# Where and in which tiles the sums of xT's quarters are made, at the seam between expert 0 and expert 1

## The chip, the cores and the metric

One core of a Trainium2 chip. The metric is the device time of the whole program in microseconds (us), lower is better. Most executions of one kernel agree within 0.3%.

## The reference

Attention with exponential features makes x (4608 x 512). A router turns x into weights P by eight alternating normalisations, and eight experts add to the output:

```python
logits = x @ w_gate
P = np.exp(logits - logits.max())
for _ in range(8):
    P /= P.sum(1, keepdims=True) + 1e-09
    P /= P.sum(0, keepdims=True) + 1e-09
    P *= N / E
out = 0
for e in range(8):
    out += P[:, e:e+1] * (np.maximum(x @ w1[e], 0) @ w2[e])    # D = 512, F = 1024
```

## The kernel before

The tokens lie in nine groups of 512. Expert 0 is computed while the attention ends and while the router runs, in plain products; its result, still without P, lies in `acc`. Experts 1 to 7 use a scheme with seven in place of eight quarter products. It needs sums of quarters: sums of the weights (once per expert), "X sums" of xT, which is x transposed (once per group, the same for all experts), and "S sums" of the hidden values hT (each group, each expert). A small scheduler written in Python inside the kernel fixes the order of every engine's instructions before the program is built. It books modelled durations, takes buffers from rings of tiles, and always issues what can start first. So a change in a ring or in a duration can move any instruction of any engine.

The X sums are made once, at the seam between expert 0 and expert 1, written to DRAM, and read back for every expert and group:

```python
ring("s_p", [128, 4, 256], BF16, "S", 5)        # S sums of hT
ring("s_p", [128, 2, 2, 256], BF16, "X", 3)     # X sums, and their reloads

def sub(eng, el, out_, x, y, op, r, w):         # dve = VectorE, pool = GpSimd
    f = nc.vector if eng is dve else nc.gpsimd
    eng(..., lambda: f.tensor_tensor(out=out_(), in0=x(), in1=y(), op=op), r, w)

def sums_x(g):
    X = [new("X") for _ in range(2)]            # two of the three X tiles
    ...
    for n, y, z, r in ((0, b12, b11, []), (1, b22, x(0), [0]), (2, b22, b12, []), (3, b21, x(1), [1])):
        sub(dve if g < 6 else pool, 512, x(n), y, z, ALU.subtract, ...)
    for i in range(2):
        dma("SP", ..., out=Xd[g][i], in_=X[i]())

def load_x(g):                                  # for every expert and group
    X = [new("X") for _ in range(2)]
    for i in range(2):
        dma("SP", ..., out=X[i](), in_=Xd[g][i])
```

The router's serial chain, eight times, nearly all on VectorE with one tiny product on TensorE:

```python
u  = L * c                        # DVE, from the second time on
rr = 1 / u.sum(experts)           # DVE reduce, DVE reciprocal
wv = L * rr                       # DVE
cs = wv.sum(tiles)                # DVE reduce
pc = colw.T @ cs                  # TensorE, 8 columns
c  = 1 / pc                       # DVE
# after the eighth: P = wv * c    # DVE
```

TensorE's second product on a bank (a buffer in which products add up) waits until ScalarE has copied the first one's partial sum out (`U`, an `activation` copy). And before expert 1 adds to a group, ScalarE must scale what expert 0 left there, four "rescales" for each of nine groups:

```python
def keep(fp, n):                                # TensorE waits for this U copy
    act(512, lambda: nc.scalar.copy(out=u[fp][n](), in_=x[fp]()), [x[fp]], [u[fp][n]])
...
if e == 1:
    for ts in range(4):                         # the rescales: can start once P is there
        act(512, lambda ts=ts: nc.scalar.activation(
            out=acc[g][:, ts, :], in_=acc[g][:, ts, :], func=ACT.Copy, bias=0.0,
            scale=P[:, 4 * g + ts, 0:1]), ["P", ("acc", g, ts)], ...)
```

## Time and profile before

| what | before |
|---|---|
| median of the first three runs | 1064.5 us (1063.76 to 1066.44) |
| span of the profiled run | 1064.0 us |
| TensorE busy, page | 96% |
| routing weights P (start of the last routing instruction) | 264.21 us |
| first product of expert 1 | 274.36 us |
| TensorE without work, 275 to 345 us | 7.83 us (70.00 - 62.17) |

The windows of the kernel before show the span cut into stages: for each engine the busy time in the window and the number of instructions, then the granted TensorE clock (1.00 is full speed), the DMA share and GB/s. PE is TensorE, PEld its weight loads, DVE VectorE, ACT ScalarE and POOL GpSimd.

```profile
core 0: us, PE busy (x) PEld busy (x) DVE busy (x) ACT busy (x) POOL busy (x), PEclk, DMA share, GB/s
225.00:240.00 15.00, 12.69 (x96) 6.20 (x95) 10.39 (x23) 2.62 (x6) 9.31 (x8) 0.89 0.19 71
240.00:275.00 35.00, 34.79 (x170) 16.76 (x172) 27.32 (x61) 19.81 (x34) 0.98 (x2) 1.00 0.34 83
275.00:290.00 15.00, 12.72 (x106) 9.94 (x105) 9.30 (x15) 15.00 (x30) 1.09 (x2) 1.00 0.53 89
290.00:305.00 15.00, 12.73 (x113) 10.75 (x112) 14.12 (x20) 13.08 (x28) 12.91 (x10) 1.00 0.32 107
305.00:325.00 20.00, 17.38 (x144) 14.50 (x143) 14.94 (x27) 9.97 (x22) 7.74 (x6) 0.91 0.31 102
325.00:345.00 20.00, 19.34 (x179) 17.18 (x177) 16.67 (x32) 11.47 (x25) 6.30 (x5) 1.00 0.21 71
...
345.00:960.00 615.00, 615.00 (x5636) 551.02 (x5634) 475.71 (x848) 386.07 (x806) 265.09 (x211) 1.00 0.27 62
```

From 345 to 960 us TensorE has no gap at all: nothing that frees another engine there can shorten the run. The gaps lie at the seam. What TensorE waited for between 275 and 345 us (line waited for, total, times, longest):

```profile
PE P_5744 L983 <- DVE S L896: 2.0, 1, 2.0
PE P_5553 L983 <- DVE S L896: 1.7, 1, 1.7
PE P_5208 L983 <- ACT U L1011: 0.8, 1, 0.8
...
```

Two S sums on VectorE are 3.7 us of it, about half of the 7.83 us without work. What VectorE did ahead of the first (its timeline: start, length, line, operation, tiles, shapes):

```profile
291.46 1.06 DVE L896 TENSOR_TENSOR X<-xT 128x512 bf16<-128x512 bf16 x1
...
293.23 1.50 DVE L896 TENSOR_TENSOR X<-xT,X 128x512 bf16<-128x512 bf16 x1
...
299.23 2.56 DVE L896 TENSOR_TENSOR S<-hT 128x1024 bf16<-128x1024 bf16 x2
```

Four X sums stand in front of expert 1's own work, and the first and the last of them take 1.06 and 1.50 us in place of 0.42. The two S sums take 2.56 us in place of the usual 1.28. GpSimd was busy with work that reads two inputs in both stretches; at 296 to 301 us that was its own four X sums, of which this is the last:

```profile
299.65 1.60 POOL L896 TENSOR_TENSOR X<-xT,X 128x512 bf16<-128x512 bf16 x1
```

Ahead of the second wait, the X sums can be read in the chain of work that ended last (start, length, engine, tile, line): four X sums, the last three of them shown, run just before the S sums that TensorE waits for. There they take their usual time, 1.33 us of the chain.

```profile
313.20 1.00 DVE X L896 x3
314.21 0.79 DVE acc_78 L1087 x2
314.99 1.21 DVE S L896 x2
316.25 1.06 PE P_5744 L983 x8
```

The second S-sum wait has a sequel. TensorE's timeline (in brackets: idle before, and what ended it):

```profile
316.25 1.05 PE L983 MATMUL P_5744<-w_3852,S 128*128 128x256 bf16 x8 [2.00 <-DVE S L896]
317.92 1.67 PE L983 MATMUL P_5735<-T,S 128*128 128x256 bf16 x7 [0.62 <-ACT V L1097]
319.39 1.06 PE L983 MATMUL P_5766<-xT,w_3831 128*128 128x256 bf16 x4
```

After the wait four products take 1.06 us where they otherwise take 0.60. In one-microsecond windows the granted clock is 0.50 from 318 to 321 us.

### The profile page before, as it was taken

To read this page: it belongs to the slowest core of one execution; us is meant where nothing else is said; L and a number is where in the kernel's file an instruction comes from. 1 tells how busy PE (TensorE), PEld (TensorE's weight loads), DVE (VectorE), ACT (ScalarE), POOL (GpSimd) and SP (SyncE) were. 2 spreads that over 40 slices of the span, in tenths; PEclk is the share of its full clock that TensorE was granted. 3 is DMA by queue.
4 is the path that set the end of the run, shared out by engine and by line. 5 is a ranking of instruction groups with operands and counts; after the bars stand their busy time and mean duration, and the time that the engine had idled before them with its cause. 6 is when DMAs were issued, how large, how long until landed. Compare 5 with 4: busy or idle time off the path is not lost.

```text
span 1064.0 us, 24542 instructions
## 1 busy us (share of the span) xinstructions
PE 1021.8 (96%) x9498; PEld 842.4 (79%) x9536; DVE 834.4 (78%) x1628; ACT 711.4 (67%) x1568; POOL 496.8 (47%) x567
## 2 busy tenths in 40 slices
PE   6789999999989999999999999999999999999997
PEld 3456666654668888888888888888888888888886
DVE  6889989978697788877867887778777777787775
ACT  5799989944965666566666666666666665666664
POOL 8775756450163444443443443444443444334434
PEclk9999999999999999999999999999999999999999
DMA  9998986812531144113411251116111621114332
GB/s 144 152 179 136 136 143 120 139 41 70 90 130 60 41 90 87 44 41 80 90 41 48 53 110 50 41 50 120 41 41 41 114 57 50 41 42 128 121 118 119
DMA packets 104948, 91.57 MB, mean 86 GB/s; under 512 B 45312, under 2 KB 80256, under 8 KB 104832
## 3 DMA queue, kind: packets, MB, share of 16 engines
q1 hardware_dynamic: 64752, 63.78, 21.9%
q0 software_dynamic: 40080, 26.23, 18.3%
q8 instruction: 74, 1.21, 0.5%
q14 instruction: 42, 0.34, 0.1%
HBM read 94.98 MB, written 14.16 MB: 103 GB/s over the span
## 4 chain that ended last, share of the span: by engine, by line
PE 86%; DVE 5%; ACT 4%; issue 2%; POOL 2%; DMA 1%; ACTq 0%; DVEq 0%; POOLq 0%
DVE m L376 1%; DVE S L896 1%; DMA qk_r<-in_q_dram 1%; DVE xb L590 0%; DVE X L896 0%; ACT U L1011 0%; ACT V L1097 0%; POOL X L896 0%; PE P_6471 L983 0%; PE P_6315 L983 0%; PE P_5735 L983 0%; PE P_16154 L983 0%; PE P_12150 L983 0%; PE P_11799 L983 0%; PE P_8771 L983 0%
## 5 line engine op out<-in xcount | busy, mean ns | idle before, releaser
L983 PEld LDWEIGHTS <-S 128*128 128x128 bf16 x2016 | 197.1, 98 | 31.9 <-DVE S L896 5.9
L983 PEld LDWEIGHTS <-T 128*128 128x128 bf16 x1512 | 147.9, 98 | 19.4 <-issue 2.0
L983 PEld LDWEIGHTS <-hT 128*128 128x128 bf16 x1512 | 147.8, 98 | 18.4 <-DVE hT L1015 1.0
L896 DVE TENSOR_TENSOR S<-hT 128x1024 bf16<-128x1024 bf16 x126 | 85.8, 717 | 0.0
L1100 POOL TENSOR_TENSOR acc_4737<-acc_4737,V 128x512 f32<-128x512 f32 x28 | 35.8, 1284 | 54.7 <-ACT V L1097 54.3
L1100 POOL TENSOR_TENSOR acc_80<-acc_80,V 128x512 f32<-128x512 f32 x28 | 35.5, 1273 | 55.2 <-ACT V L1097 54.7
L1100 POOL TENSOR_TENSOR acc_79<-acc_79,V 128x512 f32<-128x512 f32 x28 | 37.3, 1337 | 51.1 <-ACT V L1097 50.6
L1100 POOL TENSOR_TENSOR acc_77<-acc_77,V 128x512 f32<-128x512 f32 x28 | 35.8, 1289 | 52.7 <-ACT V L1097 52.4
L1100 POOL TENSOR_TENSOR acc_4740<-acc_4740,V 128x512 f32<-128x512 f32 x28 | 35.8, 1288 | 49.5 <-ACT V L1097 49.4
L1100 POOL TENSOR_TENSOR acc_78<-acc_78,V 128x512 f32<-128x512 f32 x28 | 37.2, 1336 | 45.6 <-ACT V L1097 45.5
L1100 POOL TENSOR_TENSOR acc_4738<-acc_4738,V 128x512 f32<-128x512 f32 x28 | 35.6, 1276 | 46.0 <-ACT V L1097 45.4
L1100 POOL TENSOR_TENSOR acc_81<-acc_81,V 128x512 f32<-128x512 f32 x28 | 35.6, 1275 | 45.1 <-ACT V L1097 44.4
L1100 POOL TENSOR_TENSOR acc_4739<-acc_4739,V 128x512 f32<-128x512 f32 x28 | 35.7, 1283 | 43.8 <-ACT V L1097 43.3
L384 PEld LDWEIGHTS <-hT 128*128 128x128 bf16 x288 | 27.6, 100 | 23.5 <-issue 2.2
L896 DVE TENSOR_TENSOR S<-hT,S 128x1024 bf16<-128x1024 bf16 x63 | 46.0, 730 | 0.2
L896 DVE TENSOR_TENSOR S<-S,hT 128x1024 bf16<-128x1024 bf16 x63 | 44.1, 701 | 0.8
L384 PEld LDWEIGHTS <-w_449 128*128 128x128 bf16 x288 | 26.1, 99 | 23.4 <-issue 2.9
L384 PEld LDWEIGHTS <-qkT 128*128 128x128 bf16 x256 | 23.8, 100 | 20.7 <-DVE xb_r L595 4.4
L983 PEld LDWEIGHTS <-w_3831 128*128 128x128 bf16 x288 | 28.7, 99 | 5.1 <-issue 1.1
L983 PEld LDWEIGHTS <-w_5136 128*128 128x128 bf16 x288 | 28.2, 98 | 3.3
L983 PEld LDWEIGHTS <-w_13108 128*128 128x128 bf16 x288 | 28.2, 98 | 3.3
L983 PEld LDWEIGHTS <-w_11506 128*128 128x128 bf16 x288 | 28.2, 98 | 3.3
(4013 smaller groups left out, 3303.2 us busy)
## 6 DMA issues: line engine op xcount, KB each, us to landing
v_m<-in_v_dram SPq DMA_DIRECT2D x15, 512.0 KB, 4.6
qk<-in_k_dram POOLq DMA_DIRECT2D x15, 256.0 KB, 4.9
qk<-in_q_dram POOLq DMA_DIRECT2D x15, 256.0 KB, 5.7
X<-xd_98 SPq DMA_DIRECT2D x7, 256.0 KB, 2.6
X<-xd_99 SPq DMA_DIRECT2D x7, 256.0 KB, 2.7
X<-xd_100 SPq DMA_DIRECT2D x7, 256.0 KB, 2.6
X<-xd_101 SPq DMA_DIRECT2D x7, 256.0 KB, 2.7
X<-xd_102 SPq DMA_DIRECT2D x7, 256.0 KB, 2.6
```

Source lines behind the costliest of these rows:

```text
L376: dve(el, lambda: nc.vector.tensor_reduce(out=dst(), in_=src(), axis=AX.X, op=ALU.max, apply_absolute_value=True), r, w)
L384: nc.tensor.matmul(out_, lhsT=lhsT, rhs=rhs, start=start, stop=stop)
L896: lambda: f.tensor_tensor(out=out_(), in0=x(), in1=y(), op=op), r, w, **kw)
L983: pe(256, lambda i=i, k=k, z=z: nc.tensor.matmul(bank()[:, 256 * i:256 * i + 256], lhsT=lhs(k, i), rhs=rhs(k), start=first and z, stop=k = ...
L1100: pool(670, lambda: nc.gpsimd.tensor_tensor(out=acc[g][:, 2 * i:2 * i + 2, 256 * j:256 * j + 256], in0=acc[g][:, 2 * i:2 * i + 2, 256 * j: ...
```

## The change

The intent: make the X sums in the five S tiles, which nobody needs before the first S sums of expert 1, so that the sums need not share three tiles with their own reloads; and make all of them on VectorE, where one takes 0.42 us alone, against 1.15 us on GpSimd. The core of the diff (shortened):

```diff
     def sums_x(g):
-        X = [new("X") for _ in range(2)]
+        X = [new("S") for _ in range(2)]
         def x(n):
-            return lambda: X[n // 2]()[:, n % 2]
+            return lambda: X[n // 2]()[:, n % 2 * 2:n % 2 * 2 + 2]
         ...
-            sub(dve if g < 6 else pool, 512, x(n), y, z, ALU.subtract,
+            sub(dve if g in (0,1,2,3,4,5,6,7,8) else pool, 512, x(n), y, z, ALU.subtract,
```

The cut parts of the diff give names to choices that stay as they were (a tenth group, expert 0's quarters, a plain product for the last group: all switched off), and write 18 of ScalarE's copies as activations with scale 1.0.

More of the change, by code (lines that the diff above doesn't have):

```diff
@@ L682, in akey @@
     def akey(g):
-        return ["late"] if g >= NA else []
+        return ["late"] * (g >= NA) + ["P"] * (g >= 9)
     def up0(g, part):
@@ L694, in down0, with keys @@
         py = down(W[0][1], hts[g], tss, akey(g))
+        def keys(ts):
+            return [("acc", g, ts)] + [("acc", g, ts, j) for j in range(2) if g >= 9]
         for i, ts in enumerate(tss):
             if ts % 2:
-                act(512, lambda i=i, ts=ts: nc.scalar.copy(
-                    out=acc[g][:, ts, :], in_=py()[:, 512 * i:512 * i + 512]),
-                    [(py, i)] + akey(g), [("acc", g, ts)])
-            else:
-                dve(512, lambda i=i, ts=ts: nc.vector.tensor_copy(
-                    out=acc[g][:, ts, :], in_=py()[:, 512 * i:512 * i + 512]),
-                    [(py, i)] + akey(g), [("acc", g, ts)])
+                act(512, lambda i=i, ts=ts: nc.scalar.activation(
+                    out=acc[g][:, ts, :], in_=py()[:, 512 * i:512 * i + 512], func=ACT.Copy,
+                    bias=0.0, scale=P[:, 4 * g + ts, 0:1] if g >= 9 else 1.0),
+                    [(py, i)] + akey(g), keys(ts))
+            else:
+                dve(512, lambda i=i, ts=ts: nc.vector.tensor_scalar_mul(
+                    out=acc[g][:, ts, :], in0=py()[:, 512 * i:512 * i + 512],
+                    scalar1=P[:, 4 * g + ts, 0:1]) if g >= 9 else nc.vector.tensor_copy(
+                    out=acc[g][:, ts, :], in_=py()[:, 512 * i:512 * i + 512]),
+                    [(py, i)] + akey(g), keys(ts))
     halves, rests, W = {}, {}, {}
@@ L745, in expert0 @@
     def expert0(i):
-        if i < 0 or i >= 40:
+        if i < 0 or i >= (4 * (0 or NG) + 4):
             return
         plan.prio = 0
-        if i < 36:
+        if i < (4 * (0 or NG)):
             up0(i // 4, i % 4)
@@ L866, with store @@
         expert0(i)
-    def store(g, ts):
-        if g < 8:
+    def store(g, ts, one=0):
+        if one:
+            dma('SP', 1 << 18, 320, lambda: nc.sync.dma_start(
+                out=out[g * S:g * S + SM].rearrange('(p j) d -> p j d', j=NJ)[:, ts:ts + 1],
+                in_=acc[g][:, ts:ts + 1, :]),
+                [('acc', g, ts, j) for j in range(2)], [('out', g, ts)])
+        elif g < 8:
             if ts % 2:
@@ L898, in sums_w @@
     def sums_w(e, w1, w2):
+        eng = pool if e == 0 else dve
         def q(w, i, j):
@@ L905, in k @@
         def k(w, i, j):
-            return [(w, i, j)]
+            return [(w, i, j)] if e else [(w, n) for n in range(4)]
         S = [None] + [new("T") for _ in range(3)]
@@ L919, in sums_w @@
         late = ["late"] + (["P"] if e == 1 else [])
-        sub(dve, 1024, s(2), q(w1, *a11), q(w1, *a21), ALU.subtract,
+        sub(eng, 1024, s(2), q(w1, *a11), q(w1, *a21), ALU.subtract,
             k(w1, *a11) + k(w1, *a21) + late, [S[2]])
-        sub(dve, 1024, q(w1, *a21), q(w1, *a21), q(w1, *a22), ALU.add,
+        sub(eng, 1024, q(w1, *a21), q(w1, *a21), q(w1, *a22), ALU.add,
             k(w1, *a22) + late, k(w1, *a21))
-        sub(dve, 1024, s(1), q(w1, *a21), q(w1, *a11), ALU.subtract,
+        sub(eng, 1024, s(1), q(w1, *a21), q(w1, *a11), ALU.subtract,
             k(w1, *a21) + k(w1, *a11) + late, [S[1]])
-        sub(dve, 1024, s(3), q(w1, *a12), s(1), ALU.subtract,
+        sub(eng, 1024, s(3), q(w1, *a12), s(1), ALU.subtract,
             k(w1, *a12) + [S[1]] + late, [S[3]])
         b11, b12, b21, b22 = (0, 0), (0, 1), (1, 0), (1, 1)
-        sub(dve, 1024, t(2), q(w2, *b22), q(w2, *b12), ALU.subtract,
+        sub(eng, 1024, t(2), q(w2, *b22), q(w2, *b12), ALU.subtract,
             k(w2, *b22) + k(w2, *b12) + late, [T[2]])
-        sub(dve, 1024, q(w2, *b12), q(w2, *b12), q(w2, *b11), ALU.subtract,
-            k(w2, *b11) + late, k(w2, *b12))
-        sub(dve, 1024, t(1), q(w2, *b22), q(w2, *b12), ALU.subtract,
-            k(w2, *b22) + k(w2, *b12) + late, [T[1]])
-        sub(dve, 1024, t(3), q(w2, *b21), t(1), ALU.subtract,
+        t1, t1k = q(w2, *b12), k(w2, *b12)
+        if 0 and e == E - 1:
+            T[0] = new("T")
+            t1, t1k = t(0), [T[0]]
+        sub(eng, 1024, t1, q(w2, *b12), q(w2, *b11), ALU.subtract,
+            k(w2, *b11) + k(w2, *b12) + late, t1k)
+        sub(eng, 1024, t(1), q(w2, *b22), t1, ALU.subtract, k(w2, *b22) + t1k + late, [T[1]])
+        sub(eng, 1024, t(3), q(w2, *b21), t(1), ALU.subtract,
             k(w2, *b21) + [T[1]] + late, [T[3]])
@@ L940, in sums_w @@
         Bq = {"11": (q(w2, *b11), k(w2, *b11)), "21": (q(w2, *b21), k(w2, *b21)),
-              "22": (q(w2, *b22), k(w2, *b22)), "t1": (q(w2, *b12), k(w2, *b12)),
+              "22": (q(w2, *b22), k(w2, *b22)), "t1": (t1, t1k),
               "t2": (t(1), [T[1]]), "t3": (t(2), [T[2]]), "t4": (t(3), [T[3]])}
@@ L947, in xq @@
         return lambda: xT[:, 2 * i:2 * i + 2, 512 * g + 256 * j:512 * g + 256 * j + 256]
-    Xd = [[dram.tile([128, 2, 2, 256], BF16, name=f"xd{g}{i}") for i in range(2)]
+    Xd = [[dram.tile([128, 4, 256], BF16, name=f"xd{g}{i}") for i in range(2)]
           for g in range(NG)]
     def sums_x(g):
-        X = [new("X") for _ in range(2)]
+        X = [new("S") for _ in range(2)]
         def x(n):
-            return lambda: X[n // 2]()[:, n % 2]
+            return lambda: X[n // 2]()[:, n % 2 * 2:n % 2 * 2 + 2]
         b11, b12, b21, b22 = xq(g, 0, 1), xq(g, 0, 0), xq(g, 1, 1), xq(g, 1, 0)
@@ L972, in load_x @@
         for i in range(2):
-            dma("SP", 1 << 18, 250, lambda i=i: nc.sync.dma_start(out=X[i](), in_=Xd[g][i]),
+            dma("SP", 1 << 18, 250, lambda i=i: nc.sync.dma_start(out=X[i]().rearrange("p a b c -> p (a b) c"), in_=Xd[g][i]),
                 [("Xd", g, i)], [X[i], "order of X"])
@@ L1022, in relu @@
                 func=ACT.Relu, bias=0.0, scale=1.0), [x[fp]], [(hT[i], fp, j)])
-        more = [("banks", fp) for fp in range(2)]
+        more = [("banks", 0), ("banks", 1)]
         more += [k for n in ("s2", "s3", "22") for k in A[n][1]] + X + list(r0)
@@ L1039, in w1 @@
         def w1(fp):
-            prod(w, fp, "s1", "t1", True, A["s4"][1] + list(r0), hT, [("banks", fp)])
+            prod(w, fp, "s1", "t1", True, A["s4"][1] + r0, hT, [("banks", fp)])
         def x3(fp):
@@ L1057, in up7, with acc_part, down8 @@
             for fp in range(2)}
+    def acc_part(g, i, j):
+        return lambda: acc[g][:, 2 * i:2 * i + 2, 256 * j:256 * j + 256]
+    def down8(e, g, hT, w2):
+        for ts in (2, 3, 0, 1):
+            py = new("P1")
+            for fc in range(8):
+                i, j = fc // 4, ts // 2
+                pe(512, lambda py=py, ts=ts, fc=fc: mm(
+                    py(), hT[fc // 4]()[:, fc % 4, ts * 128:ts * 128 + 128], w2()[:, fc, :],
+                    fc == 0, fc == 7), [(hT[i], fp, j) for i in range(2) for fp in range(2)]
+                    + [(w2, i, j) for i in range(2) for j in range(2)] + ["P"], [py])
+            dve(580, lambda py=py, ts=ts: nc.vector.scalar_tensor_tensor(
+                out=acc[g][:, ts, :], in0=py(), scalar=P[:, 4 * g + ts, e:e + 1],
+                in1=acc[g][:, ts, :], op0=ALU.mult, op1=ALU.add),
+                [py, "P"], [("acc", g, ts, j) for j in range(2)])
+            store(g, ts, 1)
     def down7(e, g, hT, B7):
@@ L1066, in hk @@
             return [(hT[j], fp, i) for fp in range(2)]
+        late, seen = akey(g), set()
         S = [new("S") for _ in range(4)]
@@ L1080, in prod, with start @@
             product(bank, lambda k, i: lhs()[:, k, 128 * i:128 * i + 128],
-                    lambda k: f()[:, k, :], 4, r + r2 + ["P"] + list(more), first)
+                    lambda k: f()[:, k, :], 4, r + r2 + (["P"] if e else late) + list(more), first)
+        def start(bank, i, j):
+            out_ = acc_part(g, i, j)
+            w = [("acc", g, 2 * i + n, j) for n in range(2)]
+            if (i, j) in seen:
+                dve(500, lambda: nc.vector.tensor_tensor(
+                    out=out_(), in0=bank().rearrange("p (a b) -> p a b", a=2), in1=out_(),
+                    op=ALU.add), [bank] + late, w)
+            else:
+                act(512, lambda: nc.scalar.copy(
+                    out=out_(), in_=bank().rearrange("p (a b) -> p a b", a=2)),
+                    [bank] + late, w)
+            seen.add((i, j))
         def read(bank, i, j):
+            if e == 0:
+                return start(bank, i, j)
             for n in range(2):
@@ L1093, in read2 @@
         def read2(bank, i, j):
+            if e == 0:
+                return start(bank, i, j)
             u = new("V")
@@ L1103, in read2 @@
                 [(u, 0), (u, 1)], [("acc", g, 2 * i + n, j) for n in range(2)])
-        if e == 1:
+        if e == 1 and g < 9:
             for ts in range(4):
@@ L1108, in down7 @@
                     out=acc[g][:, ts, :], in_=acc[g][:, ts, :], func=ACT.Copy, bias=0.0,
-                    scale=P[:, 4 * g + ts, 0:1]), ["P", ("acc", g, ts)],
+                    scale=P[:, 4 * g + ts, 0:1]), ["P", ("acc", g, ts)] + akey(g),
                     [("acc", g, ts, j) for j in range(2)])
@@ L1150 @@
     dn = None
-    for e in range(1, E):
-        w1, w2 = load_w(e, [("xT", 5, 3)])
-        if e == 1:
-            for g in range(NG):
+    for e in range(0 if 0 else 1, E):
+        w1, w2 = load_w(e, [("xT", 5, 3)]) if e else W[0]
+        if e == (0 if 0 else 1):
+            for g in (0,1,2,3,4,5,6,7,8):
                 sums_x(g)
         A7, B7 = sums_w(e, w1, w2)
-        for g in (list(range(NG)) if e < E - 1 else [8] + list(range(8))):
+        for g in (range(0, NG) if e == 0 else range(NG) if e < E - 1 else [8, *range(8)]):
             X = load_x(g)
@@ L1167 @@
                 dn["out"]()
-            dn = down7(e, g, hT, B7)
-    for n in ORDER:
-        if len(n) == 2:
-            dn[n]()
-    dn["out"]()
+            if 0 and e == E - 1 and g == 7:
+                down8(e, g, hT, w2)
+            else:
+                dn = down7(e, g, hT, B7)
+    if not 0:
+        for n in ORDER:
+            if len(n) == 2:
+                dn[n]()
+        dn["out"]()
     plan.run(tc)
```

## The prediction

> **What bounds the kernel now.** The busy table gives TensorE 96%, and from 340 us to 1050 us the windows show it busy without a gap. Time can be won only at the seam (225-345), where expert 0 and the serial routing chain end and expert 1's seven-product scheme begins. There the windows show:
> - TensorE idle 7.8 us between 275 and 340: 2.3 in 275-290, 2.3 in 290-305, 2.6 in 310-320, 0.7 in 335-340.
> - A granted clock of 0.77 and 0.89 in 315-325, an estimated 1.7 us more.
>
> ScalarE is busy without a pause from 265 to 295: it rescales acc in 36 instructions, 0.62 us apart, once the routing weights P are ready (264.7). TensorE's waits there name ScalarE's U copies (0.8, 0.6 us), then the S sums on VectorE (1.7 and 2.0 us). Just before these, VectorE did X sums for later groups; beside GpSimd's X sums at 296-301 two S sums took 2.56 us in place of 1.28. The Trainium skill (SBUF — State Buffer, "Who interferes with whom") says that two-input VectorE instructions contend with GpSimd's reads; the trace agrees.
>
> **What changes.** No arithmetic is added. Much of the diff is dead here (`down8`, a tenth group, expert 0's quarters). What counts:
> - 12 X sums leave GpSimd (1.15 to 1.28 us each) for VectorE (0.42 us, 0.34 apart): +4 us of VectorE.
> - The sums no longer wait for the three X tiles that reloads hold. In the built order all 36 stand inside the routing chain, before P; 16 stood between 291 and 334. From the eighth on, the write-outs go out with no reload between them.
>
> **Cost.** The chain gets 28 more VectorE sums before P. Interleaved with dependent routing steps, one costs an estimated 0.2 us beyond the spacing (two sums between reduce, reciprocal and product make it 1.25 in place of 0.90), so about 6 us, less idle gaps of some 5 us. But TensorE's tiny column-sum products stand later in its stream: the eighth comes 26 products of 0.216 us later, so P comes at about 270 in place of 264.7. Expert 0's fill keeps TensorE busy till 275 either way; only 8 rescales, in place of 15, are done before expert 1 starts. The other 28 mix with the U copies; at 21 such the loss was 2.3 us (275-290), so an estimated 3 to 3.5 us now. For waits for S tiles I allow 0.5 us.
>
> **Gain.** The S-sum waits of 300-305 and 310-320 and the clock dip (1.7 + 2.6 + 1.7 us), and some of the 0.7 at 335, go nearly all: about 6 us. Net about 4.5 us. TensorE's last 1237 rows keep their order, so the tail stays.
>
> **Prediction:** 1060.0 us, 8 in 10 within 1055.5 to 1065.0. Faster by over 2%: 0.01; within 2%: 0.97; slower by over 2%: 0.02.
>
> **Right or wrong in the profile:**
> - No GpSimd X sums; 36 X sums on VectorE, all before P.
> - P lands at 268 to 273; ScalarE saturated from there to about 300 or later.
> - TensorE idle in 275-345 falls from 7.8 to 3 to 5 us; the clock stays at 1.00 from 300 on.
>
> **What would make it wrong:** VectorE stalling in the routing chain on an S tile whose write-out hasn't landed, which stops TensorE at a column-sum product (slower); the later rescales starving the U copies well beyond 3.5 us, with a new clock dip (no gain); or the rescales being absorbed (up to 9 us faster).

## The result, and the profile after

The changed kernel: 1057.64 us median (1055.92 to 1057.87, 4 runs), before 1064.51, ratio 0.9929 (95% interval 0.9912 to 0.9946). A second set of rounds on a chip shared with other runs gave 1057.17 and 0.9922 (0.9909 to 0.9936).

| what | before | after |
|---|---|---|
| median | 1064.51 us | 1057.64 us |
| profiled span | 1064.0 us | 1055.9 us |
| P | 264.21 us | 269.17 us |
| first product of expert 1 | 274.36 us | 273.57 us |
| TensorE without work, 275 to 345 | 7.83 us | 3.19 us |
| X sums on GpSimd | 12 | 0 |

The windows of the changed kernel:

```profile
225.00:240.00 15.00, 13.54 (x104) 6.86 (x103) 12.84 (x36) 2.80 (x7) 0.00 (x0) 0.89 0.35 112
240.00:275.00 35.00, 35.00 (x180) 17.42 (x179) 30.66 (x75) 16.57 (x29) 1.71 (x2) 1.00 0.48 140
275.00:290.00 15.00, 11.89 (x103) 9.83 (x101) 10.56 (x17) 15.00 (x30) 0.18 (x1) 1.00 0.65 120
290.00:305.00 15.00, 14.94 (x138) 13.21 (x137) 10.12 (x20) 15.00 (x33) 6.67 (x6) 1.00 0.13 40
305.00:325.00 20.00, 19.98 (x184) 17.64 (x182) 15.44 (x29) 14.78 (x32) 8.30 (x7) 1.00 0.13 41
325.00:345.00 20.00, 20.00 (x186) 17.93 (x184) 13.63 (x25) 13.07 (x28) 9.64 (x8) 1.00 0.18 54
```

From 345 to 960 us TensorE is again busy for 615.00 of 615.00 us. From 290 to 345 us TensorE lost 5.6 us before and 0.08 us now, and the clock stays at 1.00. VectorE's work moved from 290-305 (14.12 to 10.12 us) to 225-275 (37.71 to 43.50 us). GpSimd has no vector work at the seam before 289 us. The price is in 275-290: ScalarE is saturated in both, but now until 310 us, and TensorE loses 3.11 us there in place of 2.28. Its waits between 275 and 345 us are now all of one kind:

```profile
PE P_5278 L999 <- ACT U L1027: 1.9, 3, 0.9
PE P_5354 L999 <- ACT U L1027: 1.2, 1, 1.2
```

ScalarE's timeline there shows why: rescales stand in front of U copies.

```profile
276.04 1.96 ACT L1162 ACTIVATE acc_79<-acc_79,P 128x512 f32<-128x512 f32 x3
277.89 0.58 ACT L1027 COPY U<-P_5278 128x512 f32<-128x512 f32 x1
```

And this is a turn of the routing chain after the change, with X sums between its steps:

```profile
252.50 0.42 DVE L907 TENSOR_TENSOR S<-xT,S 128x512 bf16<-128x512 bf16 x1
252.84 0.45 DVE L853 TENSOR_REDUCE rr<-T 128x36 f32<-128x288 f32 x1
253.20 0.41 DVE L907 TENSOR_TENSOR S<-xT 128x512 bf16<-128x512 bf16 x1
253.53 0.37 DVE L855 RECIPROCAL rr<-rr 128x36 f32<-128x36 f32 x1
253.82 0.36 DVE L907 TENSOR_TENSOR S<-xT,S 128x512 bf16<-128x512 bf16 x1
254.10 0.45 DVE L856 TENSOR_TENSOR T<-L,rr 128x288 f32<-128x288 f32 x1
```

The reduce starts at 252.84 and the product that needs its reciprocal at 254.10, 1.26 us later, with two sums inside. Without them the same two steps took 0.90 us in the kernel before. A sum of 0.41 us thus costs the chain 0.18 us, as the prediction had estimated from the few turns of the kernel before that already held sums.

### The profile page after: what moved, and what is told of

It is laid out like the page before. It is cut to its first block, busy times and chain, and to the rows that moved or that the text cites. A ratio compares the mean times of both kernels' runs of the same rounds, so it can differ in the third digit from the quotient of the medians.

```text
span 1055.9 us, 24583 instructions
## 1 busy us (share of the span) xinstructions
PE 1021.8 (97%) x9536; PEld 843.4 (80%) x9536; DVE 827.8 (78%) x1640; ACT 711.7 (67%) x1568; POOL 481.7 (46%) x555
## 4 chain that ended last, share of the span: by engine, by line
PE 87%; ACT 4%; DVE 3%; issue 1%; POOL 1%; ACTq 0%; DVEq 0%
DVE m L376 1%; ACT U L1027 1%; ACT V L1152 0%; DVE S L907 0%; PE P_16154 L999 0%; PE P_12438 L999 0%; PE P_11777 L999 0%; PE P_9602 L999 0%; PE P_9491 L999 0%; PE P_6816 L999 0%; PE P_6655 L999 0%; PE P_16045 L999 0%; PE P_15691 L999 0%; PE P_15449 L999 0%; PE P_15335 L999 0%
## 5 line engine op out<-in xcount | busy, mean ns | idle before, releaser
L907 DVE TENSOR_TENSOR S<-hT 128x1024 bf16<-128x1024 bf16 x126 | 81.5, 683 | 0.0
```

## The experiments

The diffs here are shortened; what stands in brackets is put in words. Three theories of the gain were set against each other. The place theory: VectorE's X sums leave expert 1's stage, where they delayed the S sums. The GpSimd theory: the gain comes from ending the contention between GpSimd's X sums and VectorE. The tile theory: reloads come earlier since the sums don't hold their tiles. In the fences below, where a whole line of waits has a bare P, the trace doesn't number the product's bank.

### e1_tiles_only: the tiles without the engine

```diff
-            sub(dve if g in (0,1,2,3,4,5,6,7,8) else pool, 512, ...
+            sub(dve if g < 6 else pool, 512, ...
```

> Half of the change: the X sums go into S tiles, but those of groups 6 to 8 stay on GpSimd. In the built order all 36 sums stand before P. Three theories of the gain (the changed kernel stands at 0.993 of before). Place theory (mine): VectorE's sums leave expert 1's stage, where they delayed the S sums that TensorE waits for; it expects most of the gain here, 0.993 to 0.995, no S-sum wait in 300-320, and a slower first routing step beside GpSimd's sums. GpSimd theory: the gain comes from ending the port contention between GpSimd's X sums and VectorE; it expects 0.997 to 1.000. Tile theory: the reloads come earlier because the sums no longer hold their tiles; it expects the whole gain, 0.993.

Measured: 1061.84 us, 0.9962 (0.9949 to 0.9974). Every theory missed: half the gain. The S-sum waits are gone, as the place theory said, but TensorE waits 4.3 us for U copies, and the granted clock is 0.57 in 280-285. The cause begins in the routing chain, on VectorE:

```profile
234.85 1.37 DVE L907 TENSOR_TENSOR S<-xT 128x512 bf16<-128x512 bf16 x1
...
272.76 0.46 DVE L866 TENSOR_TENSOR P<-T,c_bc 128x288 f32<-128x288 f32 x1
```

Beside GpSimd's sums (228.6 to 238.6 us) an X sum takes 1.37 us in place of 0.42, and the scheduler, which knows that the two engines share a port, also books the chain's other steps later. P comes at 272.76 us, 3.6 us after the changed kernel's, and the rescales with it. In 275-290 TensorE does 73 products where the changed kernel does 103; at 0.109 us for each that is an estimated 3.3 us, most of this run's distance to the changed kernel, and more of it comes with the lowered clock than with idle time (3.91 us idle, against 3.11). So the engine matters too. That it does so through the later P is argued from this trace; no run delays P alone.

### e2_engine_only: the engine without the tiles

```diff
 (from the kernel before)
-            sub(dve if g < 6 else pool, 512, ...
+            sub(dve, 512, ...
```

> The other half: all X sums on VectorE, but in the X tiles shared with the reloads, as before. In the built order 8 sums stand before P and 28 after it, all of them on VectorE. Place theory: little or no gain, 0.997 to 1.001, with S-sum waits left in 290-345. GpSimd theory: the whole gain, about 0.993. Tile theory: no gain, 1.000.

Measured: 1064.37 us, 0.9988 (0.9974 to 1.0002). As the place theory expected: no GpSimd sum is left, and there is little or no gain. TensorE still waits for VectorE and ScalarE (S sums 2.4 us, U 2.2, hT 1.2, V 1.0), and is without work for 6.85 us in 275-345.

```profile
PE P L983 <- DVE S L896: 2.4, 2, 1.8
```

The GpSimd theory, which expected 0.993, falls as the reason of the gain. What the contention alone costs, this run does not say: it also puts 12 more sums on VectorE behind P, and TensorE loses 1.22 us between 345 and 960 us, where the kernel before loses nothing.

### e3_late_sums: tiles and engine as changed, the place undone

```diff
-            for g in (0,1,2,3,4,5,6,7,8):
+            for g in (0, 1):
                 sums_x(g)
 ...
+            if e == 1 and g >= 2:      (only when group g-2's hT is whole)
+                sums_x(g, (every key of group g-2's hT))
             X = load_x(g)
```

> The changed kernel with one thing undone, the place: tiles and engine as changed, but the sums of group g (2 and up) may start only when group g-2's hT is whole, which puts 28 of them back between the S sums of expert 1; P comes again at about 265. Place theory: the gain goes, 0.997 to 1.001. GpSimd theory: it stays, 0.993. Tile theory: it stays nearly, 0.993 to 0.995.

Measured: 1066.66 us, 1.0011 (0.9998 to 1.0023): the whole gain is gone, although tiles and engine are the changed ones. TensorE is without work for 6.31 us in 275-345 (this view shows the products and the weight loads alone):

```profile
275.00:345.00 70.00, 63.69 (x557) 53.87 (x555) 1.00 0.30 80
```

The waits are spread otherwise than before (U 2.3 us, acc sums on VectorE 1.6, V 1.2, hT 0.6), so this run shows that the late place costs the gain; it doesn't show the same two S-sum waits again. Nor are the sums just where they were before. TensorE does 557 products in this window where the changed kernel does 603, an estimated 5.0 us at 0.109 us for each; but the gate also holds the last sums back so long that TensorE does 32 products fewer between 345 and 960 us (5604 in place of 5636), an estimated 3.5 us that neither the kernel before nor the changed one loses there. And the clock stays at 1.00 where the kernel before has its dip. So the late place costs most of the gain at the seam itself; that the time comes out equal to the kernel before is in part chance. The GpSimd and the tile theory, which both expected the gain to stay, fall. Against the tile theory this run is the weaker evidence, since a sum made late is also reloaded late; but it expected the whole gain in e1 too, and no TensorE wait in the kernel before names a reload.

### e4_rescale_priced: what is left in 275-290

```diff
-                act(512, lambda ts=ts: nc.scalar.activation(      (the rescale)
+                act(636, lambda ts=ts: nc.scalar.activation(      (booked as 0.62 us in place of 0.517)
```

> The changed kernel with one number changed: the scheduler prices a rescale of acc at 0.62 us, the measured spacing, in place of 0.517. The 3.1 us that TensorE still waits in 275-290 are, by my theory, U copies that come late because each rescale placed before them takes 0.1 us longer than planned. If so, the waits fall to 1 to 2 us and the ratio to before to about 0.991. If it is the sheer amount of ScalarE work, the waits and the ratio stay, 0.993.

Measured: 1054.92 us, 0.9899 (0.9885 to 0.9912). One number in the scheduler's book of durations is worth some 3 us. Its waits:

```profile
PE P L999 <- ACT U L1027: 1.6, 3, 0.6
```

U waits fell from 3.1 to 1.6 us, as expected. The price can be read in the trace: rescales that follow each other start 0.61 to 0.62 us apart. The Trainium skill (ScalarE: Activation LUTs, section "What ACT_TABLE_LOAD costs") gives 186 ns + 0.833 ns for each element, 93 ns more for a pointer operand, and 93 ns of overlap between neighbours. An estimate from these figures, for 512 elements with one pointer operand, is 706 ns long and 613 ns apart. The trace agrees in the spacing, and in the length where rescales follow each other (0.71 to 0.75 us; late in the stage up to 0.84). The book's 0.517 us falls 0.096 us short of that spacing, about what the page gives for the pointer operand.

### e5_late_rescale: no rescales at the seam

```diff
+        (once, after P: divide P of experts 1 to 7 by P of expert 0, all groups but 7)
-        if e == 1 and g < 9:
+        if e == 1 and g == 7:
             (rescale acc by P of expert 0)
 ...
+                    if g != 7:                       (in the last expert, just before the store)
+                        act(636, (scale acc by P of expert 0))
                     store(g, ts)
```

> The changed kernel with the 32 rescales of all groups but the last to be stored taken out of the seam: P of experts 1 to 7 is divided by P of expert 0 once (three VectorE instructions after P), and acc is scaled by P of expert 0 just before its store, in the last expert, where ScalarE has room. If the U waits left in the changed kernel (3.1 us in 275-290) come from rescales, they fall under 1 us, and the ratio to before is 0.989 to 0.991, about 3 us under the changed kernel and no worse than the priced rescale (0.9899). If P itself, 5 us later, is what TensorE waits for, the waits stay: they would name V or acc in place of U, and the ratio stays 0.993.

Measured: 1057.68 us, 0.9930 (0.9917 to 0.9943): no better than the changed kernel. The windows show a gain that was given back. First the changed kernel, then this one, from 275 us on:

```profile
275.00:345.00 70.00, 66.81 (x603) 58.61 (x601) 49.75 (x88) 57.85 (x118) 24.79 (x20) 1.00 0.26 61
...
1030.00:1055.90 25.90, 18.98 (x170) 16.23 (x167) 14.94 (x27) 11.08 (x24) 11.70 (x9) 0.99 0.31 122
```

```profile
275.00:345.00 70.00, 68.98 (x630) 61.29 (x628) 53.66 (x95) 44.66 (x92) 25.20 (x20) 1.00 0.25 61
...
960.00:1030.00 70.00, 69.53 (x630) 61.43 (x629) 50.51 (x93) 54.11 (x112) 28.67 (x23) 1.00 0.34 118
1030.00:1055.30 25.30, 16.91 (x148) 14.09 (x145) 12.54 (x24) 13.37 (x29) 10.05 (x8) 0.97 0.32 125
```

At the seam TensorE's time without work falls from 3.19 to 1.02 us and the U waits to 0.2 us: the rescales were their cause, and a P that comes at 268.28 us stops nothing by itself. But from 960 us to the end it rises from 6.92 us (all of it after 1030) to 8.86 us. The scales of the last groups hold up their V copies there: TensorE waits 1.3 us for V, a wait that the changed kernel doesn't have. My expectation had "where ScalarE has room" for the last expert, and that failed at its very end.

### e6_before_late_rescale: the same in the kernel before

The edit of e5, made in the kernel before.

> The same removal of the rescales in the kernel before, whose X sums stay where they were. Place theory: only the U waits go (1.4 us) with what follows from them; the S-sum waits (1.7 and 2.0 us) and the clock dip stay, so 0.997 to 0.999, and the distance to the changed kernel with late rescales stays 6 to 8 us. Rival: rescales and X sums are two halves of one shortage, so that either removal gives the whole gain: 0.991 to 0.993.

Measured: 1066.48 us, 1.0009 (0.9991 to 1.0027), above the 0.997 to 0.999 expected. S-sum waits stay (4.8 us), and the loss at the end, which I had not expected, takes what the seam gains, as in e5. The distance to e5 (8.8 us by the medians of the same rounds) is a little over the 6 to 8 us expected. What stays at the seam is the X sums' place.

### e7_sums_after_P: another early place

```diff
-                xkeys(g) + ["late"] + [(X[i // 2], i % 2) for i in r]
+                xkeys(g) + ["late"] + ["P"] * (g >= 2) + [(X[i // 2], i % 2) for i in r]
```

> The changed kernel, but the sums of groups 2 to 8 wait for P: they follow the routing chain at once (in the built order nearly all stand before expert 1's first S sums), so P comes at about 260 in place of 269 and no sum lies among the later S sums. It parts two readings of the place theory. If it only matters that no X sum lies among expert 1's S sums: 0.990 to 0.993, since the rescales start 9 us earlier. If VectorE has no room for them between P and expert 1's first hT sums (weights' sums, ADD of U) either: waits for hT or S in 275-300, 0.995 to 1.000.

Measured: 1061.02 us, 0.9955 (0.9944 to 0.9967). The ratio lies within the second reading, but the waits are not those it named. P comes at 259.4 us, ten before the changed kernel's, and yet U waits are 4.6 us (the longest 2.6) and hT waits 0.7 us. An early P alone does not help; 5.19 us are lost in 275-290.

### e8_change_again

> The changed kernel once more, on the chip and in the rounds of the other three, to compare with them directly: 0.993.

Measured: 1057.17 us, 0.9922 (0.9909 to 0.9936). The result stands, and the waits of the first profile are here again (U 3.0 us).

### e9_paced_rescale: the rescales spread over expert 1

```diff
-                act(512, lambda ts=ts: nc.scalar.activation(
+                act(636, lambda ts=ts: nc.scalar.activation(
 ...
-                    scale=P[:, 4 * g + ts, 0:1]), ["P", ("acc", g, ts)] + akey(g),
+                    scale=P[:, 4 * g + ts, 0:1]), ["P", ("acc", g, ts)] + akey(g) + hk(1, 1),
```

`hk(1, 1)` are the keys of a late part of the group's own hT: its rescales now come one group at a time.

> The changed kernel with the rescales of a group held until that group's own hT is nearly whole (and priced as measured), which spreads them over all of expert 1 in place of a burst after P; nothing is moved to the end. The run with late rescales emptied the seam (1.0 us idle in 275-345, U waits 0.2 us) and gave it back at the end. If the burst is the cause of the U waits, here the seam is as empty, the end is as in the changed kernel, and the ratio is 0.988 to 0.990. If spreading only moves the waits to V or acc in 290-390, 0.991 to 0.993.

Measured: 1054.58 us, 0.9899 (0.9885 to 0.9912), within the expectation, and as fast as e4. Its waits in 225-345 for ScalarE:

```profile
PE P L999 <- ACT U L1027: 0.6, 2, 0.3
```

TensorE is without work for 0.82 us in 275-345, and the end is as in the changed kernel (6.71 us from 960 on). So the seam after the change is nearly empty with either e4 or e9. These are the best kernels, 10 us under the kernel before.

### e10_after_P_paced

The edits of e7 and of e9 together.

> The sums of groups 2 to 8 after P, as in the run of that name (0.9955, U waits 4.6 us with a clock dip), with paced rescales. If that run lost to the rescale burst alone, it now equals the paced changed kernel within 0.001 (0.988 to 0.990): then what counts is only that no X sum lies among expert 1's S sums. If VectorE is short there, hT waits of 1 to 3 us stay in 275-300: 0.991 to 0.994.

Measured: 1057.11 us, 0.9924 (0.9910 to 0.9937). Not equal to e9: hT waits of 1.1 us on VectorE and one U wait of 1.1 us stay, and 2.37 us are lost in 275-290 where e9 loses 0.81. Pacing gave e7 back an estimated 3.3 us of its loss, by the ratios (the two ran in different rounds); the hT waits that remain are VectorE's, which has 13.70 us of work in those 15 us. The place inside the routing chain is the better one.

### e11_before_paced

The edit of e9, made in the kernel before.

> The kernel before with paced rescales, and the X sums where they were. The place theory expects the S-sum waits (4.8 us in the run of before with late rescales) and the clock dip to stay: 0.997 to 1.000, so that the distance to the paced changed kernel is 8 to 11 us, at least the whole gain of the change. If rescales and X sums are two halves of one shortage: 0.991 to 0.994.

Measured: 1060.31 us, 0.9957 (0.9944 to 0.9969). I missed here: pacing, with the measured price (e9's edit holds both), is worth 0.4% to the kernel before too. S-sum waits of 3.8 us stay, as the place theory says. The distance to e9 is 5.7 us, not 8 to 11; so of the change's 7 us some 6 remain when the rescales are out of the way. The clock dip in 305-325, which I had tied to the S-sum waits, is not in this profile, though the same waits of 2.0 and 0.6 us are; the dip's 1.7 to 2.0 us may be the rest, which no run settles.

### e12_before_again: is the clock dip firm?

> A second profile of the kernel before, unchanged. My prediction booked an estimated 1.7 us for a lowered granted clock in 315-325 (0.77 and 0.89), seen in one profile. If that dip follows from the S-sum wait of 2.0 us, it is here again, at the same products; if it comes and goes, the waits are the same as before to 0.1 us and the granted clock is 1.00 there, and the 1.7 us are no firm part of the gain.

Measured: 1064.16 us (one round), 0.9986 (0.9957 to 1.0015). The S-sum waits are the same (3.7 us for two). The dip at the seam is here again, 0.66 in 315-320. An earlier dip, at 230-235, which the first profile of before and that of the changed kernel share (0.89 over 225-240 in both), is absent here. The products show what the dip costs:

```profile
305.00:310.00 5.00, 5.00 (x49) 4.47 (x47) 3.51 (x8) 3.48 (x7) 1.57 (x2) 1.00 0.29 108
310.00:315.00 5.00, 3.00 (x29) 2.46 (x26) 4.96 (x13) 1.68 (x4) 0.99 (x1) 1.00 0.47 157
315.00:320.00 5.00, 4.93 (x30) 3.48 (x31) 3.25 (x2) 1.12 (x3) 2.66 (x2) 0.66 0.36 105
```

In 315-320 TensorE is busy for 4.93 us, and yet it does 30 products where a full window holds 49. At 0.109 us for each (eight take 0.87 us in the chain that ended last) that is an estimated 2.0 us lost in a window that looks full. The Trainium skill (Perfetto Trace Analysis, "Identifying the Most-Contended Engine") warns that matmul busy time is no measure of how near TensorE is to its best, and this agrees: count products.

## Why the prediction was right

The predicted time was 1060.0 us with a range of 1055.5 to 1065.0; 1057.64 lies in it, and the direction and the mechanism were right. The gain was 6.9 us by the medians (7.5 by the ratio) in place of 4.5. Point by point:

- "All 36 stand inside the routing chain, before P": so on the chip. P at 269.2 us, predicted "about 270". It was reckoned by counting products: the scheduler's order fixes where the tiny column-sum products stand in TensorE's stream, which was full from 240 us on.
- "TensorE idle in 275-345 falls from 7.8 to 3 to 5 us": 3.19. "The clock stays at 1.00 from 300 on": so.
- "An estimated 3 to 3.5 us" lost to rescales among U copies: 3.1 us of U waits. e4, e5 and e9 show that the rescales are the cause: priced, moved, or priced and paced, the waits fall to 1.6, 0.2 and 0.6 us. The good size of the estimate is in part luck: it scaled the 2.3 us lost in 275-290 before, of which only 1.4 us were U waits; the U waits themselves more than doubled.
- "ScalarE saturated from there to about 300 or later": to about 310.
- The reason of the gain, that X sums leave the stage of expert 1's S sums, is shown by e3 (place undone: no gain) with e2 (engine alone: hardly any), within the limits told there, and by the chain in the profile before. The tiles matter because they make the early place possible. No run moves VectorE's sums early and leaves GpSimd's late, so how much of the first S-sum wait was contention stays open.

The size was off in the terms of the sum:

- Gain, "about 6 us": the time without work in 290-345 fell from 5.55 to 0.08 us, and the clock dip adds the booked 1.7 (2.0 in the second profile). That is an estimated 7.2 to 7.5 us. I had left out most of the small waits for hT and V in 290-300 and 335-340, which went with the rest.
- "For waits for S tiles I allow 0.5 us": none was found. TensorE is full from 240 to 275 us (35.00 of 35.00), so no column-sum product was late enough to stop it.
- The routing stage itself was booked at nothing. From the last transposes of xT to expert 1's first product it took 46.68 us before (227.68 to 274.36) and 45.51 after (228.06 to 273.57). Both profiles hold the early clock dip; in the profiles without it the same stretch is 45.11 (e12, before) and 44.47 (e3, VectorE alone). So an estimated 0.6 to 1.2 us come from GpSimd's sums leaving this stage. Second profiles agree: 46.69 (e6) against 45.51 (e8) with the dip, 45.10 (e11) against 44.47 (e10) without. But e5 and e9, with all sums on VectorE, take 45.01, and e1, with GpSimd's sums, 45.70, so it is not settled to better than that. One piece can be seen in the kernel before: a step of the chain beside a GpSimd sum took 1.45 us in place of 0.46 (at 232.87), and TensorE stood 0.49 us before the column-sum product that followed (at 235.24; the profile names a write-out of X, but the product reads what VectorE ended at 235.04).

Together 7.2 to 7.5, less 0.8 for the rescales, and 0.6 to 1.2 more: 7.0 to 7.9 us, against 6.9 to 8.3 measured (8.3 is 0.78% of 1064.5, from the second set of rounds).

The contention was told rightly in kind. The Trainium skill (SBUF — State Buffer, "Who interferes with whom") says that a VectorE instruction with two inputs in SBUF contends with a GpSimd instruction that reads SBUF, and calls the shared pair of ports an exclusive lock. The trace agrees that they contend: in e1 an X sum grows from 0.42 to 1.37 us beside GpSimd, of 1.15 to 1.37 us itself. What it cost there seems to have been less the longer instruction than the later P, which is argued and not shown (see e1).

Open: why U waits in e7 are so long with P ten microseconds earlier. ScalarE is saturated there from 275 to 290 as in the others, VectorE is at 13.34 of 15 us, and the clock is lowered after; which of these came first, no run tells apart. That e10 regains most of the loss points to the rescales, but not to all of it.

## What to carry to other kernels

When the bottleneck engine is full nearly everywhere, look for its few gaps and ask which helper work stands in front of what it waits for there; work that is done once can go to a stretch where its engine waits anyway, such as between the dependent steps of a serial chain, where 0.41 us of work cost 0.18 us here. Then check what the chain's later end sets free at once: a burst of work that becomes ready all together should be priced as measured, or paced, because here a scheduler that believed each piece 0.1 us too short put it in front of the bottleneck's own needs. Moving the burst to the end of this program only moved the loss.

## What the Trainium skill lacked or had wrong

- TensorE: Matmul & The Clock Gate ("What's actually happening" and "HAM oscillation — how this bites in real kernels") gives the lowered clock as half of the full one, after an idle window of about 3.4 us, and warns of gaps longer than that; a further section ("A second HAM failure mode: psum-queue depth-cycling") tells of short idle times between groups of products that lower it too, without a length. The half is as measured: 0.50 from 318 to 321 us. No gap reached 3.4 us here: from 314.25 to 317.92 us TensorE was without work for 2.00 and 0.62 us, with eight products between, and the clock still fell. With the same waits (2.00 and 0.62 us, eight products between) it did not fall in the profile of e11. A page could say what share of a window must be busy.
- VectorE: DVE Perf Modes ("The DRAIN you can't avoid") has the gap after each instruction, but not what an independent instruction between two dependent ones costs: steps of the routing chain start 0.49 and 0.41 us apart alone, and 0.69 and 0.57 us apart with an independent sum between them, so that a sum of 0.41 us costs about 0.18 us.
- Perfetto Trace Analysis ("Identifying the Most-Contended Engine") says that pipelined products look smaller in the trace. In this profile, whose ends are modelled, they look longer: a product of 256 columns is recorded as 0.27 us, and the next one starts 0.109 us after it. So each wait hides an estimated 0.16 us more than the idle time shows, and a lowered clock does not show in busy time at all (4.93 of 5.00 us busy, 30 products in place of 49).
